# A recurrent memory layer on one core: mask by matmul, six ring slots for seventeen streamed weights, and moved loads and stores

## The chip, the cores and the metric

One core of a Trainium2 chip runs the whole program. The metric is the device time of one execution in microseconds. A core has five engines with queues of their own: TensorE (PE) for matmuls, VectorE (DVE), ScalarE (ACT), GpSimd (POOL) and SyncE (SP), which here only issues DMAs. Sixteen DMA engines move the data. An engine works through its queue in order; semaphores order the engines among each other.

## The reference

Two layers side by side. A is a dilated sliding-window attention over 2048 tokens of 640 features with 32 heads of 20. B, which takes most of the time, is a recurrence over 64 segments of 32 tokens; 8 memory tokens are carried from one segment to the next:

```python
for s in range(n_seg):                       # 64 segments, M = 8, seg_len = 32, H = 32, Dh = 192, Dm = 640
    h = jnp.concatenate([mem, xs], axis=1)   # 40 tokens
    q = jnp.einsum('btd,dhe->bhte', h, Wq)   # k, v likewise
    scores = jnp.einsum('bhqe,bhke->bhqk', q, k) * scale
    scores = jnp.where(mask[None, None], scores, -1000000000.0)
    p = _softmax(scores, axis=-1)
    o = jnp.einsum('bhte,hed->btd', jnp.einsum('bhqk,bhke->bhqe', p, v), Wo)
    mem = o[:, :M, :]                        # into the next segment
    outs.append(o[:, M:, :])
```

The mask is causal for the 32 tokens of the segment; memory tokens see everything. All 40 x 640 outputs of a segment hang on the memory of the segment before, so segments run one after another.

## The kernel before

Layer A runs first, with some preparation for B between its blocks (`between`). Then the parts of B that need no memory are computed for all segments at once: of the 32 tokens of a segment, 24 are projected inside the loop together with the 8 memory tokens (that makes 32 rows), and the 8 others, the "left" tokens, are projected ahead of it into DRAM scratch (qk_scr, v_scr). Then comes the loop over the 64 segments, and a tail that multiplies the left tokens' head outputs (ol_scr) by Wo.

The loop's weights are cut into 64 units of 128 x 1920 bf16 (480 KB): Q, K and V have 16 each, rows r = 0 to 3 by columns j = 0 to 3, and O has 16. 48 stay in SBUF; 16 are streamed in every segment: the units j = 3 of Q, K and V, out of the scratch ws_scr, and four O units straight from B_Wo. They go through a ring of five slots (N_RING; four in `temp`, one in `ring4`); SLOT gives the slot of each in order of use. When PE has used a unit, `done` issues on SP the load of the next unit for that slot (L575).

`SegmentLoop` takes operations in the order in which they are written (`op(engine, reads, writes, emit)`), works out which waits are needed between engines from the names read and written, and emits one loop body. Each engine's order in the loop is thus the order of the calls from L747 on. What `also` names is waited for as if written, and counts as read.

One segment, with lines:
- `proj` (L592): one row r of Q, K or V, 20 matmuls for the four column groups, 32 rows of HT (the transposed input) against 384 columns; ACT or DVE copies the result out of PSUM (L600), PE transposes it (`turn`, L612), and ACT and DVE write it into QT and KT (L618).
- `load_left` (L624): the left tokens' Q and K come from qk_scr by SP, and POOL copies the Q part into place (L625). The destination of K and the places PT and PTL lie in XL, where several short-lived pieces share space: OT[0], OT[1] (head outputs) and OL (the left tokens' head outputs) lie over QT and KT.
- `scores` (L651): t = 0 takes the heads of rows 0 and 1, t = 1 those of rows 2 and 3. `softmax_1` on DVE: scale and mask (L662), maximum (L665), difference (L666). `softmax_2` on ACT: exp (L670). `softmax_3` on DVE: sums, reciprocal, products (L673 to L679). `turn_p` transposes P (L688, L690; out by L692, L693), `pv` multiplies by V (L709, L714), `heads_out` (L721) and `left_out` (L725) copy out of PSUM.
- the store of OL for both halves by ACT's queue (L801), ahead of the last O units.
- `o_units` (L739): 16 units of 12 matmuls each, added up in Y.
- the turn: DVE adds the next segment's 24 tokens to Y in z (L804; `rows` is 1 on memory rows and 0 elsewhere), transposes z into HT (L806), ACT writes Y into z with zeros on memory rows (`toks`, L807), and ACT's queue stores z (L808). The next tokens come into z by four DMAs on SP (L756) out of x_scr, a copy of B's input.

Order of the segment's second half:

```python
    softmax_3(1)
    o_units(0, 0, 3)
    turn_p(1)
    o_units(0, 3, 5)
    pv(1)
    ...
    left_out(1)
    op("ACT", ["OT0.l", "OT1.l"] + QPARTS[0] + QPARTS[1], [], lambda s: nc.scalar.dma_start(ol_scr[:, s], OL), dma="ol")
    o_units(0, 5, 8)
    o_units(1, 0, 8)
```

Of the kernel before, what the change touches and what calls it, by code (L numbers as in the profile page):

```python
# [338 lines left out]
def part_b(ctx, tc, B_x, B_mem0, B_Wq, B_Wk, B_Wv, B_Wo, out, ident, bdf, run_a):  # L339
# [41 lines left out]
    ws_scr = {u: dram.tile([128, US], BF16, name=f"ws_{u[0]}_{u[1]}_{u[2]}") for u in streamed if u[0] != O}  # L381
    x_scr = dram.tile([n_seg + 1, SEG, Dm], BF16, name="x_scr")
# [21 lines left out]
    def between(i, ps):  # L404
        if i == 1:
            turn_left(ps)
            nc.sync.dma_start(x_scr[0:n_seg].rearrange("s t d -> (s t d)").rearrange("(p n) -> p n", p=128),
                              B_x.rearrange("b s d -> (b s d)").rearrange("(p n) -> p n", p=128))
            nc.sync.dma_start(x_scr[n_seg:n_seg + 1], x3[0:1])
# [76 lines left out]
    ring4 = keep3.tile([128, US], BF16, name="ring4")[:]  # L486
    vss += [ring4[:, 384 * k:384 * k + 384] for k in range(5)]
    z = keep3.tile([128, 160], BF16, name="z")
    z0 = z
    for g in range(4):  # L490
        nc.sync.dma_start(z0[32 * g:32 * g + NX, :], x_scr[0, 0:NX, 160 * g:160 * g + 160])
        nc.sync.dma_start(z0[32 * g + NX:32 * g + 32, :], mem2[:, 160 * g:160 * g + 160])
    left_v(3)
    ws_ring = [temp[:, US * k:US * k + US] for k in range(4)] + [ring4]
    for k in range(4):
# [8 lines left out]
    rows, toks = bdf[:, 3:4], bdf[:, 4:5]  # L504
# [6 lines left out]
    OL = XLb[:, 0:2 * KO].rearrange("p (t n) -> p t n", t=2)[:, :, 4 * PW:5 * PW]  # L511
# [12 lines left out]
    for g in range(2):  # L524
        m = mask[64 * g:64 * g + 64]
        nc.gpsimd.affine_select(out=m[:, 0:NX], in_=m[:, 0:NX], compare_op=ALU.is_ge, fill=-1e9, base=0,
                                pattern=[[-1, NX]], channel_multiplier=1)
        nc.gpsimd.affine_select(out=m[:, 32:L], in_=m[:, 32:L], compare_op=ALU.is_ge, fill=-1e9, base=-NX,
                                pattern=[[0, NL]], channel_multiplier=1)
        m = mask[64 * g + 32:64 * g + 64, :]  # L530
        nc.gpsimd.affine_select(out=m[:, 32:L], in_=m[:, 32:L], compare_op=ALU.is_ge, fill=-1e9, base=0,
# [14 lines left out]
    nc.gpsimd.memset(z[:], 0.0)  # L546
# [5 lines left out]
    QPARTS = [["Q.a0", "Q.a1", "Q.l"], ["K.a0", "K.a1", "K.l"]]  # L552

# [81 lines left out]
    def scores(t):  # L635
        Sps = logits(t)

        def emit(s):
# [9 lines left out]
            seen = set()  # L648
            last = {p[4]: n for n, p in enumerate(pl)}
            for n, (_, lo, rr, j, e, cc, hi) in enumerate(pl):  # L650
                i = MM(Sps[64 * e:64 * e + 64, 4 * rr + j, :], lhsT=XLb[lo:hi, L * (4 * cc + j):L * (4 * cc + j) + 64],  # L651
                       rhs=KT[lo:hi, 4 * cc + j], start=(e not in seen), stop=(n == last[e]),
                       tile_position=(lo, 64 * e))
                seen.add(e)
# [5 lines left out]
    def softmax_1(t):  # L660
        Sps = logits(t)
        op("DVE", [f"b{SB[t]}"], ["t1"], lambda s: V_.scalar_tensor_tensor(  # L662
            out=t1[:], in0=Sps, scalar=scale, in1=mask.unsqueeze(1).to_broadcast([128, 8, L]),
            op0=ALU.mult, op1=ALU.add))
        op("DVE", ["t1"], ["mx"], lambda s: V_.tensor_reduce(out=mx, in_=t1[:], axis=AX.X, op=ALU.max))  # L665
        op("DVE", ["t1", "mx"], ["t1"], lambda s: V_.tensor_tensor(  # L666
            t1[:], t1[:], mx.unsqueeze(2).to_broadcast([128, 8, L]), op=ALU.subtract))

    def softmax_2(t):
        op("ACT", ["t1"], ["t1"], lambda s: nc.scalar.activation(t1[:], t1[:], ACTF.Exp))  # L670
# [48 lines left out]
    def heads_out(t, j):  # L719
        e = ("ACT", "DVE")[j % 2]  # L720
        op(e, [f"b{4 + j}"], [f"OT{t}.{j}"], lambda s: COPY[e](  # L721
            OT[t][:, 6 * j:6 * j + 6], ots[j].rearrange("p r x l -> p (r x) l")[:, :, 0:32]), also=QPARTS[t])

    def left_out(t):
        op("DVE", [f"b{4 + j}" for j in range(4)], [f"OT{t}.l"], lambda s: nc.vector.tensor_copy(  # L725
            OL[:, t].rearrange("p (j a k) -> p j a k", j=4, k=NL),
# [187 lines left out]
```

## Time and profile before

| | |
|---|---|
| time, median of 4 runs | 2352.89 us (2336.99 to 2355.78) |
| the profiled execution | 2333.68 us, its span 2331.5 us |
| mean granted PE clock | 0.938 |
| busy, share of the span | PE 76%, DVE 41%, ACT 30%, POOL 2% |
| moved by DMA | 611.24 MB, mean 262 GB/s |
| first to last L804 (63 segments) | 489.3 to 2252.1 us |
| ahead of the loop, behind it | about 460 us, about 80 us |

How to read it: a row of a group or of the timeline has the line, the engine, the operation, out<-in with the program's names, shapes and a count. PE is the matmuls and PEld the weight loads; SPq and ACTq are the queues of SP and ACT when they issue DMAs. In brackets or behind "<-" stands how long the engine was idle before and what ended that. A row of a stretch of time has its length, the busy us of PE, PEld, DVE, ACT and POOL, the granted PE clock (1.00 is full), the share of time for which the DMA engines were busy, and GB/s. The chain that ended last is no help here: 76% of it is "issue", time in which the profile shows no wait, because the loop's waits compare with registers. The waits between engines are shown nevertheless, and they are used instead.

### The profile page before, as it was taken

How to read it: one execution, taken by the hardware profiler on the slowest of the kernel's cores; microseconds unless marked ns; L12 is line 12 of the kernel's file. 1: busy time of each engine (PE TensorE's matmuls, PEld its weight loads, DVE VectorE, ACT ScalarE, POOL GpSimd, SP SyncE). 2: the span in 40 equal slices, each digit the busy share in tenths (PEclk: the TensorE clock that was granted, in tenths of full speed). 3: DMA queues.
4: the chain of work that ended last, by engine and by line, in shares of the span. 5: the costliest groups of instructions: out<-in, count | busy, mean ns of one | idle time of the engine just before them, and what ended most of it. 6: DMA issues, size and time to landing. Idle time of an engine off the chain costs nothing.

```text
span 2331.5 us, 108118 instructions
## 1 busy us (share of the span) xinstructions
PE 1778.5 (76%) x45948; PEld 1120.5 (48%) x45948; DVE 963.1 (41%) x2284; ACT 689.9 (30%) x1633; POOL 50.3 (2%) x150
## 2 busy tenths in 40 slices
PE   7796858777777777877777778777777777777759
PEld 5442423345544445555544455444555544545436
DVE  3666312234444444444444444444444444444430
ACT  4342312222333222332232233332332322323321
POOL 0000000000000000000000000000000000000000
PEclk9899979889999999899999999999999999999989
DMA  8030975788988888888898888888898888988981
GB/s 230 22 99 23 194 226 176 244 270 300 311 293 305 296 288 287 294 297 304 293 311 294 288 305 291 293 305 291 295 308 300 292 298 295 313 292 291 303 312 62
DMA packets 259558, 611.24 MB, mean 262 GB/s; under 512 B 90608, under 2 KB 120432, under 8 KB 256768
## 3 DMA queue, kind: packets, MB, share of 16 engines
q1 hardware_dynamic: 223872, 591.35, 76.1%
q10 hardware_dynamic: 35648, 19.34, 2.8%
q8 instruction: 29, 0.48, 0.1%
q14 instruction: 9, 0.07, 0.0%
HBM read 573.62 MB, written 39.62 MB: 263 GB/s over the span
## 4 chain that ended last, share of the span: by engine, by line
issue 76%; PE 12%; DMA 7%; DVE 2%; ACT 1%; POOL 1%; POOLq 0%; ACTq 0%; SPq 0%; DVEq 0%
PE pq L75 3%; PE ps L444 3%; PE yp L836 2%; DMA temp<-in_B_Wk_dram 1%; DMA v_scr<-abc 1%; DMA ws<-temp 1%; POOL XL L625 1%; PE oT L162 1%; DVE pv L157 1%; PE ps L458 1%; PE po L87 1%; DMA temp<-in_B_Wo_dram 1%; DMA v_scr<-ring 1%; DMA v_scr<-t 1%; PE pp L141 0%
## 5 line engine op out<-in xcount | busy, mean ns | idle before, releaser
L592 PE MATMUL bank<-temp,XL 128*32 128x384 bf16 x3200 | 648.9, 342 | 0.0
L592 PE MATMUL bank<-w,XL 128*32 128x384 bf16 x7680 | 530.6, 347 | 50.4 <-DMA temp<-ws 49.8
L592 PE MATMUL bank<-wq,XL 128*32 128x384 bf16 x3840 | 272.8, 346 | 216.7 <-DMA temp<-ws 203.1
L600 ACT CAST abc<-bank 128x384 bf16<-128x384 f32 x512 | 239.2, 479 | 591.0 <-PE bank L592 585.8
L592 PEld LDWEIGHTS bank<-w,XL 128*32 128x32 bf16 x7680 | 244.6, 101 | 219.9 <-DMA temp<-ws 69.8
L592 PEld LDWEIGHTS bank<-temp,XL 128*32 128x32 bf16 x3200 | 282.1, 100 | 0.0
L592 PEld LDWEIGHTS bank<-wq,XL 128*32 128x32 bf16 x3840 | 115.6, 99 | 325.4 <-DMA temp<-ws 261.4
L618 DVE COPY XL<-bank 128x384 bf16<-128x384 bf16 x256 | 91.1, 356 | 351.0 <-PE bank L612 201.6
L739 PE MATMUL bank<-w,XL 128*32 128x160 bf16 x9216 | 231.5, 236 | 2.3 <-issue 2.3
L600 DVE CAST abc<-bank 128x384 bf16<-128x384 f32 x256 | 141.7, 554 | 212.8 <-PE bank L592 212.5
L651 PE MATMUL bank<-XL 128*64 128x40 bf16 (+1 forms) x4096 | 125.2, 190 | 98.0 <-POOL XL L625 98.0
L739 PEld LDWEIGHTS bank<-w,XL 128*32 128x32 bf16 x9216 | 173.3, 98 | 20.3 <-issue 4.2
L651 PEld LDWEIGHTS bank<-XL 128*64 128x64 bf16 (+1 forms) x4096 | 108.1, 114 | 141.1 <-POOL XL L625 131.3
L618 ACT COPY XL<-bank 128x384 bf16<-128x384 bf16 x256 | 122.4, 478 | 175.0 <-PE bank L612 98.9
L721 ACT CAST XL<-bank 128x192 bf16<-128x192 f32 x256 | 81.4, 318 | 230.7 <-PE bank L714 153.4
L721 DVE CAST XL<-bank 128x192 bf16<-128x192 f32 x256 | 91.2, 356 | 138.8 <-ACT XL L721 138.8
L592 PE MATMUL bank<-ring,XL 128*32 128x384 bf16 x640 | 146.5, 367 | 0.0
L612 PE MATMUL bank<-ident,abc 128*128 128x128 bf16 x1536 | 139.1, 231 | 0.0
L612 PEld LDWEIGHTS bank<-ident,abc 128*128 128x128 bf16 x1536 | 92.6, 102 | 89.2 <-issue 45.8
L662 DVE SCALAR_TENSOR_TENSOR t<-bank,XL 128x320 f32<-128x320 f32 x128 | 63.0, 492 | 117.7 <-PE bank L651 117.7
L688 PE MATMUL bank<-ident,t 128*128 128x128 bf16 x256 | 36.8, 226 | 62.8 <-DVE t L679 62.8
L625 POOL COPY XL<-XL 128x192 bf16<-128x192 bf16 x128 | 44.4, 347 | 1747.3 <-DMA XL<-qk_scr 1747.3
(111 smaller groups left out, 2041.3 us busy)
## 6 DMA issues: line engine op xcount, KB each, us to landing
temp<-ws SPq DMA_DIRECT2D x644, 480.0 KB, 5.0
temp<-in_B_Wo_dram SPq DMA_DIRECT2D x196, 480.0 KB, 5.2
ring<-ws SPq DMA_DIRECT2D x129, 480.0 KB, 6.1
ring<-in_B_Wo_dram SPq DMA_DIRECT2D x64, 480.0 KB, 4.0
qk_scr<-st SPq DMA_DIRECT2D x2, 6144.0 KB, 17.3
XL<-qk_scr SPq DMA_DIRECT2D x128, 96.0 KB, 4.3
abc<-v_scr SPq DMA_DIRECT2D x64, 96.0 KB, 4.0
ol_scr<-XL ACTq DMA_DIRECT2D x64, 96.0 KB, 6.7
```

Source lines behind the costliest of these rows:

```text
L75: nc.tensor.matmul(pq[32 * dd:32 * dd + 32, :], lhsT=w[:, 4 * c + dd, :], rhs=xT[:, dc, :], start=(dc == 0), stop=(dc == 4), tile_position ...
L444: nc.tensor.matmul(ps[:], lhsT=w[:, dc, o:o + 128], rhs=XL[:, dc], start=(dc == 0), stop=(dc == 4))
L592: i = MM(ps[32 * j:32 * j + 32, :], lhsT=HT[:, dc, :], rhs=ws[j][:, dc, :], start=(dc == 0), stop=(dc == 4), tile_position=(0, 32 * j))
L600: op(e, [f"b{b}"], [f"abc{k}"], lambda s: COPY[e](ABC[k], bank[b][:, 0:384]))
L612: i = nc.tensor.transpose(tp[ty][:, c], ABC[nat[ty, r]][:, 128 * c:128 * c + 128], ident)
L618: op(e, [("b3", "b5")[ty]], [QPARTS[ty][h]], lambda s: COPY[e](QT[:, 12 * h:12 * h + 12, 0:32] if ty == Q else KT[:, 12 * h:12 * h + 12, 0:4],
L625: op("POOL", ["PT", "PTL"], ["Q.l"], lambda s: nc.gpsimd.tensor_copy(QT[:, :, 32:L], ql))
L651: i = MM(Sps[64 * e:64 * e + 64, 4 * rr + j, :], lhsT=XLb[lo:hi, L * (4 * cc + j):L * (4 * cc + j) + 64], rhs=KT[lo:hi, 4 * cc + j], start ...
L662: op("DVE", [f"b{SB[t]}"], ["t1"], lambda s: V_.scalar_tensor_tensor(out=t1[:], in0=Sps, scalar=scale, in1=mask.unsqueeze(1).to_broadcast( ...
L721: op(e, [f"b{4 + j}"], [f"OT{t}.{j}"], lambda s: COPY[e](OT[t][:, 6 * j:6 * j + 6], ots[j].rearrange("p r x l -> p (r x) l")[:, :, 0:32]), ...
L739: i = MM(Y[32 * g:32 * g + 32], lhsT=OT[t][:, 6 * j + 3 * rr + x], rhs=w[:, x, 160 * g:160 * g + 160], start=(t == 0 and n == 0 and x == 0 ...
L836: nc.tensor.matmul(yp[h][:], lhsT=OL[tb][:, 24 * (r // 2) + 6 * j + 3 * (r % 2) + x].rearrange("p s l -> p (s l)"), rhs=w[:, x, 320 * h:32 ...
```

## The change

- Mask: a matmul of the identity with the mask (its fill divided by scale) writes the mask into the scores' PSUM ahead of the products; the DVE operation of L662 goes, maximum and difference read PSUM, and exp gets scale.
- Ring: six slots and 17 streamed units (12 of Q, K, V and five of O, another choice of them); one O unit fewer stays in SBUF. ws_scr's rows stand 4096 instead of 3840 bytes apart.
- OL: the first half stays in XL and is stored behind V of row 3, the second half lies in t1 and is stored alone. `OPARTS` leaves K's left part out of what OT[1] waits for.
- Order: `load_left(0)` moves to the front of the segment, `load_left(1)` behind the first scores, five O units stand ahead of turn_p(1) and three behind it.
- z: x_scr holds the tokens in z's layout with zeros on memory rows, one DMA per segment loads it, ACT copies Y as it is (`toks` goes), and SP stores z.

```diff
-    streamed = [u for u in order if u[0] != O and u[2] == 3 or u in ((O, 0, 2), (O, 0, 3), (O, 2, 1), (O, 2, 3))]
-    N_STR, N_RING = 16, 5
-    SLOT = [0, 1, 2, 3, 0, 4, 1, 2, 0, 3, 4, 1, 0, 2, 3, 4]
+    streamed = [u for u in order if u[0] != O and u[2] == 3 or u in ((O, 1, 0), (O, 0, 3), (O, 2, 0), (O, 2, 2), (O, 3, 3))]
+    N_STR, N_RING = 17, 6
+    SLOT = [0, 1, 2, 3, 4, 5, 0, 2, 1, 3, 4, 0, 2, 1, 3, 4, 5]
...
-    ws_scr = {u: dram.tile([128, US], BF16, name=f"ws_{u[0]}_{u[1]}_{u[2]}") for u in streamed if u[0] != O}
-    x_scr = dram.tile([n_seg + 1, SEG, Dm], BF16, name="x_scr")
+    ws_scr = {u: dram.tile([128, 2048], BF16, name=f"ws_{u[0]}_{u[1]}_{u[2]}")[:, 0:US] for u in streamed if u[0] != O}
+    x_scr = dram.tile([n_seg + 1, 128, 160], BF16, name="x_scr")
...
+            zero = lx.tile([n_seg + 1, NL * 160], BF16, name="zero")
+            nc.gpsimd.memset(zero[:], 0.0)
+            for g in range(4):
+                nc.sync.dma_start(x_scr[0:n_seg, 32 * g:32 * g + NX, :], x3[:, 0:NX, 160 * g:160 * g + 160])
+                nc.sync.dma_start(x_scr[n_seg:n_seg + 1, 32 * g:32 * g + NX, :], x3[0:1, 0:NX, 160 * g:160 * g + 160])
+                nc.scalar.dma_start(x_scr[:, 32 * g + NX:32 * g + 32, :].rearrange("s t n -> s (t n)"), zero[:])
...
-    OL = XLb[:, 0:2 * KO].rearrange("p (t n) -> p t n", t=2)[:, :, 4 * PW:5 * PW]
+    OL = [XLb[:, 4 * PW:5 * PW], t1b[:, 256:256 + PW]]
...
+            for e in range(2):
+                h = slice(64 * e, 64 * e + 64)
+                MM(Sps[h], lhsT=ident[h, h], rhs=mask[h].unsqueeze(1).to_broadcast([64, 8, L]), start=True, stop=False,
+                   tile_position=(64 * e, 64 * e), skip_group_check=True)
...
-        op("DVE", [f"b{SB[t]}"], ["t1"], lambda s: V_.scalar_tensor_tensor(
-            out=t1[:], in0=Sps, scalar=scale, in1=mask.unsqueeze(1).to_broadcast([128, 8, L]),
-            op0=ALU.mult, op1=ALU.add))
-        op("DVE", ["t1"], ["mx"], lambda s: V_.tensor_reduce(out=mx, in_=t1[:], axis=AX.X, op=ALU.max))
+        op("DVE", [f"b{SB[t]}"], ["mx"], lambda s: V_.tensor_reduce(out=mx, in_=Sps, axis=AX.X, op=ALU.max))
...
+    load_left(0)
     qk(Q, 0)
     qk(K, 0)
     qk(Q, 1)
-    load_left(0)
...
+    op("SP", [], ["z"], lambda s: nc.sync.dma_start(z[:], x_scr[s + 1]), dma="xz")
     qk(K, 2)
     scores(0)
+    load_left(1)
     softmax_1(0)
     qk(Q, 3)
-    load_left(1)
...
+    op("ACT", ["OT0.l"] + QPARTS[0], [], lambda s: nc.scalar.dma_start(ol_scr[:, s, 0], OL[0]), dma="ol0")
     softmax_3(1)
-    o_units(0, 0, 3)
+    o_units(0, 0, 5)
     turn_p(1)
-    o_units(0, 3, 5)
+    o_units(0, 5, 8)
     pv(1)
...
+    op("ACT", ["OT1.l", "t1"], [], lambda s: nc.scalar.dma_start(ol_scr[:, s, 1], OL[1]), dma="ol1")
-    o_units(0, 5, 8)
     o_units(1, 0, 8)
...
-    op("ACT", ["b2"], ZG, lambda s: nc.scalar.activation(z[:], Y, ACTF.Copy, scale=toks))
-    op("ACT", ZG, [], lambda s: nc.scalar.dma_start(out3[s], z[:]), dma="yo")
+    op("ACT", ["b2"], ["z"], lambda s: nc.scalar.copy(z[:], Y))
+    op("SP", ["z"], [], lambda s: nc.sync.dma_start(out3[s], z[:]), dma="yo")
```

More of the change, by code (lines that the diff above doesn't have):

```diff
@@ L502, in part_b @@
     psum = lctx.enter_context(tc.tile_pool(name="b_ps", bufs=1, space=PSUM))
-    rows, toks = bdf[:, 3:4], bdf[:, 4:5]
+    rows = bdf[:, 3:4]
     XLb = XL[:].rearrange("p c s l -> p (c s l)")
@@ L545, in part_b @@
     nc.vector.transpose(HT.rearrange("p c t -> p (c t)"), z[:])
-    nc.gpsimd.memset(z[:], 0.0)
     lp = SegmentLoop(nc, tc, n_seg)
@@ L552, in part_b @@
     QPARTS = [["Q.a0", "Q.a1", "Q.l"], ["K.a0", "K.a1", "K.l"]]
+    OPARTS = [QPARTS[0], QPARTS[1][:2]]
     def source(u):
@@ L651, in emit @@
                 i = MM(Sps[64 * e:64 * e + 64, 4 * rr + j, :], lhsT=XLb[lo:hi, L * (4 * cc + j):L * (4 * cc + j) + 64],
-                       rhs=KT[lo:hi, 4 * cc + j], start=(e not in seen), stop=(n == last[e]),
-                       tile_position=(lo, 64 * e))
-                seen.add(e)
+                       rhs=KT[lo:hi, 4 * cc + j], start=False, stop=(n == last[e]),
+                       tile_position=(lo, 64 * e), skip_group_check=True)
             return i
@@ L742, in emit @@
                 return i
-            op("PE", [f"OT{t}.{j}", wkey(u)] + QPARTS[t], ["b2"], emit)
+            op("PE", [f"OT{t}.{j}", wkey(u)] + OPARTS[t], ["b2"], emit)
             done([u])
-    ZG = [f"z.{g}" for g in range(4)]
+    load_left(0)
     qk(Q, 0)
@@ L754, in part_b @@
     qk(K, 1)
-    for g in range(4):
-        op("SP", [], [ZG[g]], lambda s, g=g: nc.sync.dma_start(
-            z[32 * g:32 * g + NX, :], x_scr[s + 1, 0:NX, 160 * g:160 * g + 160]), dma="xz")
     qk(Q, 2)
```

44 lines of the change are left out of this document (19 added, 25 removed).

## The prediction

> **What bounds the kernel now.** First I read how long one turn of the loop takes. The row of the line that ends a segment (count, shortest/median/longest ns, first and last start), the engines' busy time between those two starts, and the answer on waits for the same stretch:
>
> ```profile
> L804 DVE SCALAR_TENSOR_TENSOR z<-bank,bdf,z x64: 382/384/386, 489.3 to 2252.1; 128x160 bf16<-128x160 f32 x64
> 489.30:2252.10 1762.80, 1347.74 (x42210) 884.68 (x42210) 754.06 (x2017) 532.00 (x1323) 43.73 (x126) 0.95 0.87 297
> PE bank L592 <- DMA temp<-ws: 252.9, 207, 2.6
> PE bank L651 <- POOL XL L625: 94.9, 98, 2.4
> PE bank L688 <- DVE t L679: 61.6, 52, 1.2
> PE bank L592 <- DVE XL L806: 4.2, 4, 1.0
> ```
>
> Between the first and the last L804 lie 63 segments: 1762.8/63 = **27.98 us** each. The first engine column is PE: 1347.74/63 = 21.39 us busy; the four waits are 413.6/63 = 6.57 us, and the two make up the segment. So PE is the thread to follow: it is never idle for another reason, and a saving counts only if it comes out of these 6.57 us: 4.08 for loads (with the 4.2 of L806), 1.51 for the 8 "left" tokens, 0.98 for the softmax. DVE (12.0 us) and ACT (8.4) are no bound. DMA is: its share is 0.87 at 297 GB/s, so a segment moves 297 x 27.98 = 8.31 MB.
>
> Part of the 4.08 us isn't a load at all. At a segment's turn (start, us taken, engine, line, idle before):
>
> ```profile
> 1216.73 0.38 DVE L804 SCALAR_TENSOR_TENSOR z<-bank,bdf,z 128x160 bf16<-128x160 f32 x1 [0.77 <-PE bank L739]
> 1217.15 0.34 DVE L806 STREAM_TRANSPOSE XL<-z 128x160 bf16<-128x160 bf16 x1
> 1217.62 0.34 PE L592 MATMUL bank<-wq,XL 128*32 128x384 bf16 x3 [1.04 <-DVE XL L806]
> ```
>
> Y, the add, the transpose and Q of row 0 are one chain of 1.04 us; the change leaves it. So 3.04 us per segment are real waits for loads. Then I looked at who holds the loads up, in SyncE's queue of the next segment and its waits, with two DMA stretches:
>
> ```profile
> 1216.14 0.39 ACTq L801 DMA_DIRECT2D ol_scr<-XL  x1
> 1218.65 2.23 SPq L575 DMA_DIRECT2D temp<-ws  x3
> 1223.66 0.58 SPq L624 DMA_DIRECT2D XL<-qk_scr  x1
> 1224.38 0.50 SPq L575 DMA_DIRECT2D temp<-ws  x1
> 1226.67 1.84 SPq L756 DMA_DIRECT2D z<-x_scr  x4
> SPq L624 <- DMA ol_scr<-XL: 80.0, 55, 2.5
> 1227.50:1229.50 2.00, 1.87 (x53) 1.32 (x54) 0.85 (x2) 0.00 (x0) 0.08 (x1) 1.00 0.16 40
> 1238.50:1239.50 1.00, 1.00 (x45) 0.78 (x37) 0.62 (x3) 0.75 (x3) 0.00 (x0) 1.00 0.10 38
> ```
>
> The store of OL (L801) is issued when the segment is nearly over, and the next segment's left load (L624) may not overwrite its source. It goes out at 1223.66, and the weight load queued behind it at 1224.38. Three microseconds later the DMA engines stand at 0.16 for 2 us. At 1238.5 they are empty again because all five slots are full and wait for PE. Every such hole is paid back at the next dense stretch, as waits of PE.
>
> **The change, part by part.** *Left loads and OL.* OL splits: its first half is stored after V, its second half lies in t1, so no Q/K destination waits for the store, and the left loads go ahead of Q of row 0 and right behind the first scores.
>
> ```profile
> 1200.47 0.94 PE L651 MATMUL bank<-XL 128*64 128x40 bf16 x32 [0.74 <-POOL XL L625]
> 1201.34 0.34 PE L592 MATMUL bank<-wq,XL 128*32 128x384 bf16 x3
> 1201.51 0.33 PE L592 MATMUL bank<-wq,XL 128*32 128x384 bf16 x3
> 1202.89 0.58 SPq L624 DMA_DIRECT2D XL<-qk_scr  x1
> 1207.00 0.35 POOL L625 COPY XL<-XL 128x192 bf16<-128x192 bf16 x1 [6.58 <-DMA XL<-qk_scr]
> 1207.40 0.94 PE L651 MATMUL bank<-XL 128*64 128x40 bf16 x32 [1.24 <-POOL XL L625]
> ```
>
> The second load has 1207.00 - 1202.89 = 4.11 us until POOL copies, and 0.40 more until PE. Issued at about 1201.6, behind the scores instead of Q of row 3, it lets PE start at 1206.1; PE would be ready at 1207.40 - 1.24 = 1206.16. The first gains several us. So 1.51 falls to about 0.1: **-1.4**. Its bounds are -1.5 and the rival below in which the loads land late.
>
> *Softmax and order.* The mask goes into PSUM by PE, DVE loses L662, and five instead of three O units stand ahead of turn_p(1), three instead of two ahead of pv(1), none between pv(1) and the second half.
>
> ```profile
> 1208.38 0.49 DVE L662 SCALAR_TENSOR_TENSOR t<-bank,XL 128x320 f32<-128x320 f32 x1 [0.77 <-PE bank L651]
> 1208.90 0.49 DVE L665 TENSOR_REDUCE XL<-t 128x8 f32<-128x320 f32 x1
> 1213.78 0.40 PE L714 MATMUL bank<-XL,abc 32*64 32x32 bf16 x24
> 1214.25 0.32 ACT L721 CAST XL<-bank 128x192 bf16<-128x192 f32 x1 [0.98 <-PE bank L714]
> 1214.54 0.80 PE L739 MATMUL bank<-w,XL 128*32 128x160 bf16 x36
> 1215.16 0.38 PE L739 MATMUL bank<-temp,XL 128*32 128x160 bf16 x12
> ```
>
> L662 and its hand-over are 0.52 us (1208.90 - 1208.38); a unit is (1215.16 - 1214.54)/3 = 0.21, two are 0.41. Together 0.93 of the 0.98 us for L679. But the units behind pv(1) covered ACT's copy: pv ends at 1214.18, the copy at 1214.57, and with 0.13 of hand-over (as from 1217.49 to 1217.62 above) PE will stand 0.52 us there. Net **-0.4** (bounds: -0.98, and +0.1 if DVE is slower on PSUM; L662 read PSUM at the same 0.49, so I see no reason).
>
> *Mask by PE.* Two 64x64 matmuls of 320 columns per scores. The nearest rows are the projections: four 384-column matmuls on four column groups start every 1201.51 - 1201.34 = 0.17 us. Side by side a pair costs 320/384 x 0.17 = 0.14, one behind another 0.28. I take 0.17: **+0.35** per segment (0.28 to 0.56).
>
> *Six slots and a seventeenth unit.* What moves now (sizes, median us to landing) and what the engines reach when they have work:
>
> ```profile
> temp<-ws SPq DMA_DIRECT2D x644, 480.0 KB, 5.0
> temp<-in_B_Wo_dram SPq DMA_DIRECT2D x196, 480.0 KB, 5.2
> ring<-ws SPq DMA_DIRECT2D x129, 480.0 KB, 6.1
> ring<-in_B_Wo_dram SPq DMA_DIRECT2D x64, 480.0 KB, 4.0
> XL<-qk_scr SPq DMA_DIRECT2D x128, 96.0 KB, 4.3
> 1192.50:1196.50 4.00, 2.37 (x46) 1.22 (x46) 1.36 (x3) 0.96 (x2) 0.00 (x0) 1.00 1.01 395
> 1231.50:1238.50 7.00, 5.20 (x177) 3.54 (x181) 3.30 (x10) 1.57 (x4) 0.35 (x1) 1.00 0.97 362
> ```
>
> The 1033 loads are 16 per segment and nine outside. One more is 0.49 MB: 8.31 becomes 8.80 MB. At 395 GB/s that takes 22.3 us, at 362 (seven us with the small transfers in it) 24.3. PE alone, with no wait for a load, would need 27.98 - 3.04 - 1.4 - 0.4 + 0.35 - 0.2 (the clock, below) = 23.3 us. So **DMA becomes the bound, just ahead of PE.** Six slots for 17 units mean each waits 6/17 of a segment between refills, against 5/16 now: at 24.8 us the same 8.75 us that it has today. I take 24.3 plus 0.2 of collisions: 1.2 us of load waits stay, **-1.85**.
>
> *SyncE's queue.* The store of z moves from ACT to SP and waits there for ACT's copy at the turn; behind it stand the left load and the load that Q of row 0 frees. That one goes out about 0.7 us later and has over 5 us until row 3 needs it: nothing. The z load is one instead of four DMAs (1.84 us of SP) and waits for the store to land; behind it is O33's load, needed last. Nothing, up to +0.3.
>
> *The clock.* Two stretches, the granted clock third from the end:
>
> ```profile
> 1132.80:1160.80 28.00, 20.90 (x707) 13.96 (x700) 12.28 (x33) 8.49 (x22) 0.69 (x2) 1.00 0.88 300
> 1104.90:1132.80 27.90, 22.87 (x602) 13.79 (x594) 11.12 (x30) 8.11 (x20) 0.69 (x2) 0.82 0.85 283
> ```
>
> At full clock PE needs 20.90 us for the same work, against the mean of 21.39. With less idle I take **-0.2** of that 0.5. The Trainium skill (TensorE: Matmul & The Clock Gate, Part 1: The HAM clock gate) says that the gate opens with activity and halves the clock after an idle window; by it nearly all of the 0.5 us would go, and the sum would be some 20 us lower.
>
> *Outside the loop.* x_scr is written in rows of 320 bytes by eight DMAs plus four of zeros on ACT, in a stretch where DMA idles:
>
> ```profile
> 60.00:100.00 40.00, 29.49 (x177) 11.64 (x177) 26.13 (x18) 11.65 (x20) 0.00 (x0) 0.79 0.02 9
> PE yp L836 <- ACT w L829: 20.5, 1, 20.5
> ```
>
> I count 0 (-5 for fewer z loads ahead of the loop, +10 if SP or ACT is held). The tail's fifth O unit loads under the 20.5 us that PE waits there for OL.
>
> **Sum:** 27.98 - 1.4 - 0.4 + 0.35 - 1.85 - 0.2 = 24.5 us; 3.48 x 64 = 223 us off the profiled execution's 2333.68 (span and launch), 2111. The median of the runs, 2352.89, is 1.0082 times that: **2128 us**.
>
> **The rivals.** (Times in the scale of the median.)
> - *The ring hides all* (0.15): 23.3 us a segment, 300 us less, 2050. For it: DMA reached 395. Against: only in stretches of 4 us.
> - *The seventeenth unit eats what the ring gives* (0.18): the 3.04 us of load waits stay; 27.98 - 1.4 - 0.4 + 0.35 - 0.2 = 26.3, 105 us less, 2246. For it: four DMAs in flight to the same engines, landing 5 us after issue.
> - *DMA is full already* (0.08), the slower side: if 297 GB/s is what this mixture can do, 8.80 MB take 29.6 us, 106 us more, 2459. It decides from a rate below 8.80/27.98 = 315 GB/s. Against: the holes at 0.10 and 0.16, which are no limit of DMA.
> - *The left load lands late* (0.07): it stands in SP's ring behind weight loads issued earlier, more of them than now. Three more at 0.49 MB/395 = 1.24 us and it lands 8.0 us after issue, 2.9 beyond its cover: 27.4, 37 us less, 2315. Near no change.
> - *Padded rows read slower* (0.02). ws_scr rows go from 3840 to 4096 bytes apart, 13 of 17 units. At half the rate 13 x 1.24 = 16 us more per segment, over 3000 us. No row of before has such a pitch. The Trainium skill (DMA: Bandwidth & Descriptors, Latency and other measured facts) speaks against powers of two as pitch, from 512 KiB up, 207 GB/s against 214 and 103 at worst; 4 KiB isn't in its list, and by its smallest figure this would be some 35 us.
>
> **How the numbers follow.** The forecast has 0.5. Its own range is 24.5 +- 0.8, 2075 to 2180. The range holds it and the two faster and weaker cases: 2035 to 2260; outside are part of the first rival and the last three. Changes under 1% can't be told from none here. Faster by more: 0.50 + 0.15 + 0.18 and part of the late left load, 0.86; slower 0.10; between 0.04.
>
> **What would show it.** L651 waits for POOL below 0.2 us a segment; no wait of L618 or L624 for ol_scr; L688's wait gone, and a new one at the first O unit behind pv(1) of about 0.5; DMA near 360 GB/s with a share over 0.93; load waits of 1.2 us beside the turn. Wrong it would be if the share rose while GB/s didn't, or if SP stood at the store or load of z for over 1 us with weight loads behind it.

## The result: 2206 us, 5.9% faster, and the profile after

| | before | after |
|---|---|---|
| median of the runs | 2344.67 us (15 runs, 2327.49 to 2368.93) | 2205.83 us (10 runs, 2202.37 to 2214.37) |
| ratio, 95% interval | | 0.9415 [0.9389, 0.9440] |
| the profiled execution | 2333.68 us | 2209.42 us, its span 2207.4 us |
| one segment | 27.98 us | 25.80 us |

The forecast was 2128 us, in a range of 2035 to 2260. The sign and the range hold. The gain is 139 us where 225 was forecast. For e10 below, the four slowest of its ten executions (2342.74 to 2354.82 us) are left out of the time, and since its profile is of the slowest of them, its rows are an upper end.

The same rows as before, now of the kernel after. First the row of the line that ends a segment (L804 before, L803 now), by line:

```profile
L803 DVE SCALAR_TENSOR_TENSOR z<-bank,bdf,z x64: 383/384/384, 498.0 to 2123.1; 128x160 bf16<-128x160 f32 x64
```

Then the stretch between its first and its last start (length, busy us of PE, PEld, DVE, ACT and POOL, granted clock, DMA share, GB/s):

```profile
498.00:2123.10 1625.10, 1343.96 (x42462) 897.54 (x42462) 709.36 (x1890) 529.30 (x1323) 43.96 (x126) 0.97 0.95 342
```

And PE's waits in it (line and what it waited for: us in all, times, longest):

```profile
PE bank L595 <- DMA temp<-ws: 95.2, 118, 1.8
PE bank L653 <- POOL XL L628: 66.7, 75, 1.3
PE bank L595 <- DVE XL L805: 62.5, 61, 1.0
PE bank L741 <- ACT XL L723: 32.4, 63, 0.5
PE bank L690 <- DVE t L681: 17.3, 42, 0.4
PE bank L595 <- DMA ring<-ws: 4.9, 14, 1.1
```

1625.1/63 = 25.80 us per segment. PE is busy for 21.33 of it, so the two kernels need the same PE time; what went is waiting. The loads' rows fell from 252.9 to 100.1 us (95.2 and 4.9) and the softmax's from 61.6 to 17.3. A new row appeared (L741, 32.4), the copy behind pv(1). The row of the turn, L805, shows its whole 62.5 us now, since no load hides it any more. But the row that the forecast had nearly gone, the left tokens by way of POOL, only fell from 94.9 to 66.7.

SyncE's queue shows where that comes from. The timeline of SP around the second left load (L627) of a segment, then POOL's copy and PE's first matmul with what arrived:

```profile
1201.88 0.37 SPq L578 DMA_DIRECT2D ring<-in_B_Wo_dram  x1
1203.01 0.57 SPq L627 DMA_DIRECT2D XL<-qk_scr  x1
...
1209.88 0.35 POOL L628 COPY XL<-XL 128x192 bf16<-128x192 bf16 x1 [8.29 <-DMA XL<-qk_scr]
...
1210.28 0.32 PE L653 MATMUL bank<-XL,ident 64*64 64x320 bf16 x2 [1.10 <-POOL XL L628]
```

The left load goes out right behind the load of O(3,3), the unit that is needed last of all, and takes 6.87 us until POOL copies. PE stood ready at 1209.18 (1210.28 - 1.10); with 0.40 from the copy to PE, a landing by 1208.78, 5.77 us after issue, would have cost nothing. The DMA answer and two stretches of the same segment:

```profile
ring<-ws SPq DMA_DIRECT2D x194, 480.0 KB, 6.3
XL<-qk_scr SPq DMA_DIRECT2D x128, 96.0 KB, 5.4
```

```profile
1202.00:1212.00 10.00, 7.44 (x233) 4.92 (x233) 4.54 (x12) 3.00 (x7) 0.35 (x1) 1.00 1.03 401
1213.00:1215.00 2.00, 2.00 (x32) 0.95 (x28) 1.55 (x6) 1.16 (x3) 0.00 (x0) 0.50 0.28 86
```

A left load of 96 KB takes 5.4 us now, against 4.3 before, because it is issued into a stretch in which the engines are full (share 1.03, 401 GB/s). One microsecond after that stretch the same engines stand at 0.28: SP issues no load from 1209.29 to 1213.97, since no slot comes free. So the transfer that PE waits for runs beside transfers that nobody needs yet, and then there is nothing to move. The granted clock in that second stretch is 0.50: a projection's matmuls start every 0.32 us there (1213.07, 1213.39), against 0.17 at full clock (1203.30, 1203.47). So PE, which has just waited, also empties the slots at half the pace.

### The profile page after: what moved, and what is told of

Read it like the earlier page. It is cut to its first block, busy times and chain, and to the rows that moved or that the text cites. A ratio compares the mean times of both kernels' runs of the same rounds, so it can differ in the third digit from the quotient of the medians.

```text
span 2207.4 us, 108320 instructions
## 1 busy us (share of the span) xinstructions
PE 1776.8 (80%) x46204; PEld 1138.2 (52%) x46204; DVE 917.6 (42%) x2155; ACT 687.4 (31%) x1633; POOL 51.3 (2%) x150
## 4 chain that ended last, share of the span: by engine, by line
issue 43%; PE 24%; DMA 22%; ACT 4%; DVE 4%; POOL 2%; ACTq 1%; SPq 0%; POOLq 0%; DVEq 0%
DMA ol_scr<-XL 13%; PE bank L595 5%; PE pq L75 3%; PE bank L657 3%; PE yp L835 2%; PE ps L447 2%; DMA temp<-ws 2%; POOL XL L628 2%; DMA w<-in_B_Wv_dram 2%; PE bank L711 2%; DMA v_scr<-abc 2%; DMA w<-in_B_Wk_dram 1%; PE ps L461 1%; DVE pv L157 1%; PE po L87 1%
## 5 line engine op out<-in xcount | busy, mean ns | idle before, releaser
L595 PE MATMUL bank<-temp,XL 128*32 128x384 bf16 x2880 | 568.3, 340 | 0.0
L595 PEld LDWEIGHTS bank<-w,XL 128*32 128x32 bf16 x7680 | 247.2, 101 | 235.8 <-DMA temp<-ws 89.3
L595 PE MATMUL bank<-wq,XL 128*32 128x384 bf16 x3840 | 255.4, 329 | 107.6 <-DVE XL L805 62.5
L595 PEld LDWEIGHTS bank<-temp,XL 128*32 128x32 bf16 x2880 | 259.3, 99 | 0.0
L741 PE MATMUL bank<-w,XL 128*32 128x160 bf16 x8448 | 216.9, 235 | 0.0
L595 PE MATMUL bank<-ring,XL 128*32 128x384 bf16 x960 | 204.4, 347 | 0.0
L741 PEld LDWEIGHTS bank<-w,XL 128*32 128x32 bf16 x8448 | 163.7, 98 | 17.9 <-issue 4.5
L615 PE MATMUL bank<-ident,abc 128*128 128x128 bf16 x1536 | 131.9, 223 | 0.0
L667 DVE TENSOR_REDUCE XL<-bank 128x8 f32<-128x320 f32 x128 | 62.9, 492 | 108.8 <-PE bank L657 108.8
L741 PE MATMUL bank<-temp,XL 128*32 128x160 bf16 x2304 | 74.9, 236 | 34.0 <-ACT XL L723 34.0
L653 PE MATMUL bank<-XL,ident 64*64 64x320 bf16 x256 | 41.4, 320 | 67.8 <-POOL XL L628 66.9
```

The lines of the kernel that those rows point to most:

```text
L595: i = MM(ps[32 * j:32 * j + 32, :], lhsT=HT[:, dc, :], rhs=ws[j][:, dc, :], start=(dc == 0), stop=(dc == 4), tile_position=(0, 32 * j))
L615: i = nc.tensor.transpose(tp[ty][:, c], ABC[nat[ty, r]][:, 128 * c:128 * c + 128], ident)
L667: op("DVE", [f"b{SB[t]}"], ["mx"], lambda s: V_.tensor_reduce(out=mx, in_=Sps, axis=AX.X, op=ALU.max))
L741: i = MM(Y[32 * g:32 * g + 32], lhsT=OT[t][:, 6 * j + 3 * rr + x], rhs=w[:, x, 160 * g:160 * g + 160], start=(t == 0 and n == 0 and x == 0 ...
```

## The experiments

**The theories.** A: the loop is bound by DMA's bytes, 8.80 MB per segment, and a byte saved is time saved. B: the order in the queues and the distances in the ring set the waits; bytes matter only through them. A2 says of B that O(3,3)'s load ahead of the left load is the one that matters, and C that it is the number of units between two uses of a slot.

All variants below carry one more instruction on POOL and on PE ahead of the left tokens' work and the scores, and their wait registers start 4096 higher. e0 is the kernel after with only that, and **each variant is read against e0**. The lines of the variants are one to six higher than in the kernel after. The variants ran in three groups (e0, e1, e3, e4; then e2, e5, e7, e8; then e6, e9, e10, e11), in which the kernel before had medians of 2330.08, 2339.63 and 2335.08 us; so differences of some 0.4% between groups say nothing.

### e0: the control

```diff
-                    E[e].reg_mov(regs[key], total[p])
+                    E[e].reg_mov(regs[key], total[p] + 4096)
...
+                    if waits[n] and (eng == 'POOL' or eng == 'PE' and 'scores' in emit.__qualname__):
+                        E[eng].sem_inc(spare[eng], 1)
```

> The changed kernel itself; only, in the loop, an increment of an unused semaphore stands between the waits and the first instruction of scores and of POOL's copy, and the registers that waits compare with start 4096 higher. It is the base for the other variants. Expected by every theory: the changed kernel's 2206 us within 0.5%, since two increments of some 0.05 us per segment on PE are 6 us at most.

Measured: 2226.84 us, 0.9541 [0.9477, 0.9606] of before; 26.02 us per segment. Its stretch and its waits:

```profile
502.60:2141.80 1639.20, 1350.45 (x42462) 904.21 (x42462) 709.15 (x1891) 527.95 (x1323) 43.73 (x126) 0.96 0.94 339
```

```profile
PE bank L598 <- DMA temp<-ws: 90.1, 114, 1.9
PE bank L656 <- POOL XL L631: 79.2, 84, 1.4
PE bank L693 <- DVE t L684: 16.9, 41, 0.4
```

It is 21 us (0.95%) over the kernel after, outside the 0.5% that was expected; PE's busy time is up by 6.5 us and the wait for the left tokens by 12.5. Which of the added instructions does it isn't known. The picture is the same, so it serves as the base.

### e4: O(3,3) loaded later

```diff
-    def done(us):
+    def done(us, late=False):
...
-            if u in pos:
+            if u in pos and (late or u != (K, 2, 3)):
...
     proj(V, 1)
+    done([(K, 2, 3)], late=True)
```

The bytes stay. Only the refill of the slot that K of row 2 frees goes out behind V of row 1, no longer ahead of the left load.

> The changed kernel with one load moved: the load of O unit (3,3), which is needed last in the segment, is issued behind V of row 1 instead of behind K of row 2, so out of the dense stretch of Q and K and into the stretch in which the DMA engines run empty. Theory A2 (bound by DMA in the dense stretch, while it stands idle later in the segment): 1.0 us a segment less, 64 us, about 2140 us, left and load waits both smaller. Theory A1 (bound by the mean rate of DMA): 2206, no change. Rival B (order of left loads behind weights): the left load has one weight load fewer ahead of it, 1.2 us earlier, its wait goes, 0.9 us a segment, 2150; then the waits for weight loads stay as they are.

Measured: 2139.22 us, 0.9169 [0.9107, 0.9232]; 24.61 us per segment. Its stretch, its waits, and SP and POOL at the second left load:

```profile
500.80:2051.20 1550.40, 1313.39 (x42462) 883.18 (x42462) 709.10 (x1891) 520.16 (x1323) 44.03 (x126) 0.99 0.99 359
```

```profile
PE bank L598 <- DMA temp<-ws: 102.7, 140, 1.4
PE bank L598 <- DVE XL L809: 62.8, 61, 1.0
...
PE bank L656 <- POOL XL L631: 6.0, 17, 0.7
```

```profile
1199.63 0.57 SPq L630 DMA_DIRECT2D XL<-qk_scr  x1
...
1205.40 0.35 POOL L631 COPY XL<-XL 128x192 bf16<-128x192 bf16 x1 [7.28 <-DMA XL<-qk_scr]
1207.61 2.98 SPq L581 DMA_DIRECT2D ring<-in_B_Wo_dram  x2
```

One load, issued 8 us behind the left load and no longer 1.1 us ahead of it, takes 88 us off the time. The left load reaches POOL in 5.77 us, and its wait falls from 79.2 to 6.0 us in all, 1.16 us per segment. PE's busy time falls by 37.1 us, 0.59 per segment, with the clock at 0.99 instead of 0.96. The load waits stay (102.7 against 90.1). A2 has the time, but not its smaller load waits. B has both waits right, and its 2150 us lies inside the interval as well. With the share at 0.99 the engines have no hole left: 359 GB/s x 24.61 us = 8.83 MB, the bytes of the forecast. This is the fastest version here that computes the whole output. It beats both kernels, and comes within 0.11 us of the segment (24.5 us) and 3 GB/s of the rate (362) that the prediction worked out for the change itself. The edit takes the load out of the queue ahead of the left load and out of the dense stretch at once; which of the two counts isn't separated here.

### e1: sixteen units, six slots

```diff
-    streamed = [u for u in order if u[0] != O and u[2] == 3 or u in ((O, 1, 0), (O, 0, 3), (O, 2, 0), (O, 2, 2), (O, 3, 3))]
-    N_STR, N_RING = 17, 6
-    SLOT = [0, 1, 2, 3, 4, 5, 0, 2, 1, 3, 4, 0, 2, 1, 3, 4, 5]
+    streamed = [u for u in order if u[0] != O and u[2] == 3 or u in ((O, 1, 0), (O, 0, 3), (O, 2, 0), (O, 2, 2))]
+    N_STR, N_RING = 16, 6
+    SLOT = [0, 1, 2, 3, 4, 5, 0, 2, 1, 3, 4, 0, 2, 1, 3, 4]
...
+        if u == (O, 3, 3):
+            res[u] = res[O, 3, 2]
...
```

O(3,3) isn't loaded; O(3,2) stands in for it.

> The changed kernel with 16 streamed units in six slots: the last O unit (3,3) isn't loaded; the product uses the resident unit (3,2) in its place, so the output differs there. 0.49 MB per segment less to move. Theory A (the DMA engines are the bound at about 342 GB/s): 0.49/342 = 1.43 us a segment less, 92 us, so about 2115 us. Rival B (PE waits for order: the left loads behind weight loads in SP's queue, and the turn; the amount of bytes matters little): the left and load waits stay, at most 0.3 us a segment less, 2185 us or more.

Measured: 2159.35 us, 0.9255 [0.9183, 0.9327]; 24.95 us per segment. Stretch and waits:

```profile
502.60:2074.30 1571.70, 1326.29 (x42462) 897.61 (x42462) 708.54 (x1891) 527.96 (x1323) 43.73 (x126) 0.98 0.93 334
```

```profile
PE bank L659 <- POOL XL L634: 77.5, 63, 1.4
...
PE bank L601 <- DMA temp<-ws: 47.5, 73, 1.5
```

67 us less, between the theories. The load waits halve (90.1 to 47.5), so bytes seem to count; but slot 5 now holds one unit alone, which also gives K of row 2 a whole segment for its load. The wait for the left tokens stays (77.5), although O(3,3) is gone: slot 5 is now refilled with K of row 2 for the next segment, from the same place in the queue. e4, with all the bytes, is 20 us faster. Both edits at once weren't tried.

### e3: left loads from ACT's queue

```diff
-        op("SP", [], ["K.l", "PT", "PTL"], lambda s: nc.sync.dma_start(left, qk_scr[:, :, t, s, :]), dma="qkl")
+        op("ACT", [], ["K.l", "PT", "PTL"], lambda s: nc.scalar.dma_start(left, qk_scr[:, :, t, s, :]), dma="qkl")
```

> The changed kernel with both left loads issued from ACT's queue instead of SP's, at the same places of the program. Theory A (DMA is the bound): the left loads land earlier, the 1.06 us for which PE waits on POOL fall to 0.3 or less, but the same bytes are moved and the weight loads come later by as much; 2195 us, within 1% of the control. Rival B (the queue order is the fault): 0.8 us a segment less, 51 us, about 2155 us.

Measured: 2249.31 us, 0.9646 [0.9575, 0.9718]. Both expectations were too low. Waits of PE, and the DMA row of the left loads (5.3 us in e0):

```profile
PE bank L656 <- POOL XL L631: 148.2, 85, 2.8
...
PE bank L598 <- DMA temp<-ws: 28.0, 57, 1.1
```

```profile
XL<-qk_scr ACTq DMA_DIRECT2D x128, 96.0 KB, 6.3
```

Another queue doesn't let the left load pass. It lands later (6.3 us), the wait for it nearly doubles, and the weight loads gain most of what it loses (90.1 to 28.0).

### e2: the old ring in the new kernel

```diff
-    N_STR, N_RING = 17, 6
-    SLOT = [0, 1, 2, 3, 4, 5, 0, 2, 1, 3, 4, 0, 2, 1, 3, 4, 5]
+    N_STR, N_RING = 16, 5
+    SLOT = [0, 1, 2, 3, 0, 4, 1, 2, 0, 3, 4, 1, 0, 2, 3, 4]
...
```

The four streamed O units are those of before too.

> The control with the old ring: five slots and the old 16 streamed units, all else as changed. One unit less to move (the 16 units in six slots took 67 us off the control), but one slot fewer. Theory A2 (bound by DMA in the dense stretch, and there what is queued ahead of the left loads and of Q3 and K3 decides): the old slots load no unit in the dense stretch that isn't needed soon, so the ring's seventeenth unit brought little; 2190 to 2230 us. Rival (the sixth slot is the gain of the change): 26.3 us a segment or more as in the prediction's second rival, 2260 us or more.

Measured: 2329.68 us, 0.9966 [0.9934, 0.9999]; 27.81 us per segment. A2's 2190 to 2230 is missed by 100 us, and the rival holds. So everything in the change but the ring is worth 0.17 us per segment by itself (0.39 with the 0.22 by which e0's segment is longer than that of the kernel after), where the prediction's steps for it add up to 1.65. Stretch, waits, and the timeline at the worst of them, Q of row 2:

```profile
497.20:2249.50 1752.30, 1420.19 (x42462) 922.43 (x42462) 704.87 (x1890) 523.86 (x1323) 43.73 (x126) 0.92 0.89 300
```

```profile
PE bank L598 <- DMA temp<-ws: 232.6, 103, 4.4
...
PE bank L693 <- DVE t L684: 22.9, 57, 0.4
...
PE bank L656 <- POOL XL L631: 6.4, 20, 0.7
```

```profile
1221.98 0.59 SPq L630 DMA_DIRECT2D XL<-qk_scr  x1
1222.70 2.76 SPq L581 DMA_DIRECT2D temp<-ws  x4
...
1227.24 0.34 PE L598 MATMUL bank<-wq,XL 128*32 128x384 bf16 x3 [2.14 <-DMA temp<-ws]
```

The waits for the left tokens and for the softmax go (6.4 and 22.9 us), as forecast, and the load wait stays: 232.6 us, against 252.9 in the kernel before. All in all PE is idle for less: 1752.30 - 1420.19 = 332 us, where it was 1762.80 - 1347.74 = 415, so 1.32 us per segment are saved. What takes them back is PE's busy time, 1.15 us per segment more than before: 0.38 for the mask (e8), and 0.77 with the clock at 0.92 instead of 0.95. That isn't chance: the mean granted clock of e2's ten executions is 0.905 to 0.914, and of the thirteen of the kernel before beside them 0.935 to 0.952.

Why the load wait stays: in the old ring Q of row 2 uses the slot that Q of row 0 has just left, four units earlier. Its load, the first of the four at 1222.70, can't go out before that, and stands behind the left load, which this change moved to the segment's front. PE is there first, whatever else became quicker. The load waits are fewer than before and longer (103 of 2.3 us on average against 207 of 1.2).

### e9: six slots, short distances

```diff
-    SLOT = [0, 1, 2, 3, 4, 5, 0, 2, 1, 3, 4, 0, 2, 1, 3, 4, 5]
+    SLOT = [0, 1, 2, 3, 0, 4, 1, 2, 0, 3, 4, 1, 5, 2, 3, 4, 5]
```

The 17 units and six slots stay, with the old reuse in the Q and K part (four units from Q of row 0 to Q of row 2, against five or more in the change).

> The control with 17 units and six slots, but the slots of Q, K and V as in the old ring: slot 0 is used again after four units (Q of row 0, Q of row 2, V of row 0) instead of five or more, and slot 5 holds two O units. As many bytes and slots as the control; only the distance between two uses of a slot in the dense stretch differs. Theory C (what decides is the distance: a load takes 5 to 6 us from issue to landing, longer than PE takes for the four units in between, which also is why the old ring gave 2330): about 27.5 us a segment, 2300 us or more, with PE waiting at Q of row 2. Rival (the number of slots, so the capacity, is what the ring brings): 2227 us within 1%.

Measured: 2371.66 us, 1.0172 [1.0097, 1.0247]: the whole gain of the change is gone. One segment is 28.35 us. Waits, and PE at the fifth projection of a segment that began at 1215.69:

```profile
PE bank L598 <- DMA temp<-ws: 153.8, 64, 4.8
PE bank L744 <- DMA ring<-in_B_Wo_dram: 92.4, 63, 2.5
```

```profile
1222.93 0.34 PE L598 MATMUL bank<-wq,XL 128*32 128x384 bf16 x3 [1.80 <-DMA temp<-ws]
```

C holds. With the same bytes, the same number of slots and the same order of work on PE, the list of slots alone is worth 145 us against e0: 1.40 us per segment of waits, and 0.93 of PE's busy time at a clock of 0.93 instead of 0.96. Part of it is a second short distance that I had overlooked: O(1,0) and O(3,3) share slot 5 four streamed units apart, the 92.4 us. The list also sets when each refill can go out, so the distance and the place in SP's queue change together.

### e5: a quarter of the bytes

```diff
-                op("SP", [], [wkey(u)], lambda s, u=u, k=k: nc.sync.dma_start(ws_ring[slot(u)], source(streamed[k])), dma=wkey(u))
+                op("SP", [], [wkey(u)], lambda s, u=u, k=k: nc.sync.dma_start(ws_ring[slot(u)][:, 0:480], source(streamed[k])[:, 0:480]), dma=wkey(u))
```

Three quarters of every streamed unit stay as they were; the number of DMAs is the same.

> The control with every streamed load in the loop cut to a quarter of its columns (480 of 1920; the rest of a slot keeps what was there, so the output differs). As many DMAs, rows and waits, a quarter of the weight bytes. Theory A2: the load waits (1.52 us a segment) and the left waits (1.26) go, and the clock rises; about 22.9 us a segment instead of 26.0, 200 us less, about 2030 us. Rival B (order of issue and waits, not bytes): at most 1 us a segment less, 2165 us or more.

Measured: 1979.34 us, 0.8465 [0.8413, 0.8517]; 22.24 us per segment. Its stretch, and the row of the left loads:

```profile
495.40:1896.50 1401.10, 1278.03 (x42462) 887.62 (x42462) 703.85 (x1891) 519.22 (x1323) 43.74 (x126) 1.00 0.41 115
```

```profile
XL<-qk_scr SPq DMA_DIRECT2D x128, 96.0 KB, 2.4
```

All of PE's waits:

```profile
PE bank L598 <- DVE XL L808: 65.0, 63, 1.0
PE bank L744 <- ACT XL L726: 32.2, 63, 0.5
PE bank L693 <- DVE t L684: 25.9, 63, 0.4
```

No wait for a load or for the left tokens is left; the left loads land in 2.4 us. So with this number of DMAs and semaphores PE needn't wait, and the bytes make the waits that e0 has. The time is 50 us below A2's 2030, and rival B is out. PE's own chain is 22.24 us, below the 23.3 that the prediction gave it, mostly since the clock stays at 1.00: PE is busy for 20.29 us, where 21.54 were forecast.

### e7 and e11: the old order of the O units

```diff
-    o_units(0, 0, 5)
+    o_units(0, 0, 3)
     turn_p(1)
-    o_units(0, 5, 8)
+    o_units(0, 3, 5)
     pv(1)
...
+    o_units(0, 5, 8)
     o_units(1, 0, 8)
```

> The control with the O units in their old places: three ahead of turn_p(1), two behind it, three behind pv(1). By the prediction's step the wait for the softmax grows by 0.41 us (from 0.27) and the wait behind pv(1) of 0.51 goes: together -0.1 us a segment, 2220 us, no difference that can be told. If the order was a gain of its own, +0.4 us a segment, 2253 us.

> Two variants in one: the load of O unit (3,3) behind V of row 1 (2139 us alone) and the O units in their old places (2215 us alone, 12 below the control). If PE's own chain still counts, 8 to 12 us less than with the moved load alone, about 2129 us; theory A2 with the DMA engines now busy for nearly all of the time: 2139, no difference.

Measured: e7 2214.94 us, 0.9468 [0.9410, 0.9525], no difference from e0 that the intervals tell; e11, this edit on top of e4, 2151.42 us, 0.9233 [0.9191, 0.9276], none from e4. The one median is 12 us lower than its base, the other, for which 2129 or 2139 was expected, 12 us higher. The softmax's row of e7:

```profile
PE bank L693 <- DVE t L684: 35.6, 43, 0.8
```

It rises from 16.9 to 35.6, and the 32 us behind pv(1) go. The order exchanges one wait for another.

### e8: the mask by DVE again

The diff is the mask's part of the change, reversed: two matmuls per scores go, and DVE has its multiply-add back.

> The control with the mask back on DVE: no matmul of the mask, scale and mask by one more DVE operation ahead of the maximum. By the prediction's step DVE's chain is 0.52 us longer and PE has 0.35 us less work: the wait for the softmax grows from 0.27 to about 0.8; +0.2 us a segment, 2240 us. Theory A2 with DMA as the bound: much of it is hidden, 2227 to 2240. If the mask by PE was a loss: 2205.

Measured: 2229.67 us, 0.9520 [0.9458, 0.9581], as e0. Its stretch:

```profile
500.30:2144.80 1644.50, 1326.25 (x42210) 898.00 (x42210) 762.72 (x2016) 527.61 (x1323) 44.01 (x126) 0.96 0.94 338
```

PE is busy for (1350.45 - 1326.25)/63 = 0.38 us less per segment, and the time is the same, since PE waits 0.47 us longer. Half of that is the softmax's row, which rises from 16.9 to 31.6 us because DVE has its operation back:

```profile
PE bank L694 <- DVE t L685: 31.6, 42, 0.8
```

Of the three forecasts 2205 is out; 2240 and "hidden" can't be told apart within this interval.

### e6: the old row pitch

```diff
-    ws_scr = {u: dram.tile([128, 2048], BF16, name=f"ws_{u[0]}_{u[1]}_{u[2]}")[:, 0:US] for u in streamed if u[0] != O}
+    ws_scr = {u: dram.tile([128, US], BF16, name=f"ws_{u[0]}_{u[1]}_{u[2]}") for u in streamed if u[0] != O}
```

> The control with ws_scr's rows 3840 bytes apart again. If the padding changes nothing in how rows are read: 2227 us within 0.5%. If padded rows read slower, as the prediction's last rival has it, 20 us less or more; if faster, 2245 or more.

Measured: 2230.03 us, 0.9553 [0.9507, 0.9599], as e0. Between rows 4096 and 3840 bytes apart no difference shows. The Trainium skill (DMA: Bandwidth & Descriptors, Latency and other measured facts) warns of powers of two as pitch from 512 KiB up; at 4 KiB this run shows nothing of it.

### e10: the old path of z

```diff
-    op("SP", ["z"], [], lambda s: nc.sync.dma_start(out3[s], z[:]), dma="yo")
...
+    op("ACT", ZG, [], lambda s: nc.scalar.dma_start(out3[s], z[:]), dma="yo")
```

With it come back the plain x_scr, four z loads per segment and the scaling of Y by `toks`.

> The control with the path of z undone: x_scr as a plain copy of the input, four z loads per segment, zeros written by ACT, the store of z from ACT's queue. The prediction counted 0 for the loop and 0 (-5 to +10) outside it. By the two profiles the loop starts some 9 us later with the change and the rest of the loop is unmoved: about 2219 us here, 8 less than the control. If the store and load of z on SP hold up weight loads, 20 us less or more than that; if the four loads were a cost, 2240 or more.

Measured: 2327.08 us as the median of six executions, 0.9956 [0.9907, 1.0005]. That is 100 us above e0, where 2219 had been expected: the widest miss of all. SP's wait at the z load (33.4 us in the kernel before, 6.0 after), PE's for the left tokens, then ACT and SP in one segment:

```profile
SPq L763 <- DMA out_dram<-z: 168.0, 59, 4.5
```

```profile
PE bank L654 <- POOL XL L629: 204.7, 63, 5.1
```

```profile
1202.07 0.57 ACTq L811 DMA_DIRECT2D out_dram<-z  x1
...
1211.59 1.84 SPq L763 DMA_DIRECT2D z<-x_scr  x4
1213.54 0.37 SPq L579 DMA_DIRECT2D ring<-in_B_Wo_dram  x1
1214.15 0.58 SPq L628 DMA_DIRECT2D XL<-qk_scr  x1
```

The z load may overwrite z only when the store has landed. The store, 40 KB from ACT's queue, holds it until 1211.59, 9.5 us after its issue, and behind the z load stand O(3,3)'s load and the left load. The row tells that the store is what SP waits for; its queue and the four-part load weren't undone one by one, so their shares stay open.

## Why the prediction was right and wrong, by its own steps

Per segment, from the rows of the kernel after:

| step | forecast | measured |
|---|---|---|
| left tokens (1.51 before) | 0.1 | 66.7/63 = 1.06 |
| waits for loads, without the turn's 1.04 (3.04 before) | 1.2 | (95.2 + 4.9 + 62.5)/63 - 1.04 = 1.54 |
| softmax and the new wait behind pv(1) (0.98 before) | 0.05 + 0.52 | 0.27 + 0.51 |
| mask by PE | +0.35 | +0.38 (e8) |
| PE busy, mask and clock in it | 21.54 | 21.33 |
| segment | 24.5 | 25.80 |
| outside the loop, in all | 0 | +13.6 |

**The step that failed is the left load's**, 0.96 of the 1.3 us. It gave the second load the 4.11 us that it had before, at an earlier place in the queue, and priced its landing at before's load. In the same text the ring was made to fill the engines, and the two steps were never put together: a fuller ring makes every landing longer, 5.4 us in place of 4.3, and O(3,3)'s new load stands right in front. The rival "the left load lands late" named the mechanism. Its size was wrong: 8.0 us to landing, where the second load reached POOL after 6.87 us in the segment shown. By its own rows its cover was 1206.16 - 0.40 - 1201.6 = 4.2 us, so that 8.0 would lie 3.8 beyond it and not 2.9. e4 moves O(3,3)'s load and leaves 6.0 us of this wait, e5 cuts the bytes and leaves none; e2, with the old ring, brings the step's whole (94.9 - 6.4)/63 = 1.40 us. So the step holds beside the old ring, where the left loads land in 3.6 us and PE, held by weight loads, also comes later; with the fuller ring most of it is lost.

**Load waits** (1.54 for 1.2): near the mark for the change, but not for the reason given. "DMA becomes the bound at 362 GB/s" is what e4 reaches; the kernel after gets 342, since its engines still run dry (0.28) behind the stretch in which PE waited for one late transfer. The prediction's count of slots, 6/17 of a segment each, was the wrong measure. e9 has the same count and takes 145 us more: what counts is how many streamed units lie between two uses of a slot, where they are fewest.

**Softmax and order**: the waits fell by 0.2 where 0.4 was forecast; the 0.52 behind pv(1) came as 0.51. In e7 and e11 the order is worth nothing that can be measured. **Mask**: +0.35 was right as PE time. With the 0.52 us that it takes off DVE's chain the forecast for the mask as a whole was a gain of 0.17 us per segment, 11 us in all, which is less than e8 can show. Both steps were summed as if PE were the only thread, although the same text had just made DMA the bound; whether DMA hides them, e8 and e11 leave open.

**The sum itself** is the second thing to correct. The steps aren't additive: e2 removes the left and softmax waits and gains 0.17 to 0.39 us, where 1.65 was forecast for all but the ring. Its waits do fall, by 1.32 us; but the load waits, which stay, come in fewer and longer pieces, and the granted clock falls with it. That the clock could go down with a step was in no term of the sum.

**The rivals on the ring**: the seventeenth unit has a price (67 us, e1) but doesn't eat all that the ring gives, and the ring can't hide everything, as 359 GB/s at a share of 0.99 (e4) leaves the engines no more room.

**The clock**: -0.2 was forecast, out of 0.5 us that were to be had. Both were too small. The prediction's two stretches don't hold the same work (707 and 602 matmuls, where a segment of the kernel before has 42210/63 = 670). In e5, at 1.00 throughout, PE is busy for 20.29 - 0.38 = 19.91 us without the mask, so of the 21.39 before, 1.48 us belonged to the clock. In the kernel after 0.44 of them came (21.33 - 0.38 = 20.95), in e4, at 0.99, 0.92, and in e2, at 0.92, PE lost 0.77. The Trainium skill's rule (TensorE: Matmul & The Clock Gate, Part 1: The HAM clock gate) says that activity opens the gate and an idle window closes it. That the clock rises as waits go, as in e4 and e5, agrees with it better than my 0.2 does. How long an idle window has to be, these rows don't show: in the kernel after, PE has no wait over 1.8 us. The sum of the waits isn't what decides, though: PE was idle for 6.59 us per segment at 0.95 before, and for 5.27 at 0.92 in e2. The longest single wait orders these kernels better: 1.0 us in e5 (1.00), 1.4 in e4 (0.99), 1.8 after (0.97), 2.6 before (0.95), 4.4 in e2 (0.92) and 4.8 in e9 (0.93); e11, with 2.5 at 0.98, doesn't fit as well. No run changes the length of a wait alone, so this is a pattern and not a shown cause.

**SyncE's queue at nothing**: its waits at the new place of z's store are as forecast, 0.79 us per segment for ACT's copy and next to nothing at the z load:

```profile
SPq L807 <- ACT z L806: 49.7, 63, 0.8
SPq L760 <- DMA out_dram<-z: 6.0, 16, 0.5
```

Whether those 0.79 us cost PE anything, no run tells. That the old path of z would have cost 100 us with the fuller ring (e10) I had not seen. **Padded rows**: refuted as a rival, by e6.

**Outside the loop** the first L803 is 498.0 - 489.3 = 8.7 us later than before, and the tail 84.3 us (2123.1 to 2207.4) against 79.4. The tail's part is at its second unit, O(1,0), now streamed:

```profile
2149.66 1.76 PE L835 MATMUL yp<-temp,w 128*128 128x320 bf16 x6 [3.83 <-DMA temp<-in_B_Wo_dram]
```

The forecast hid this load behind PE's wait for OL; PE waits 3.83 us for it, of the 4.9 us by which the tail grew. The 8.7 us ahead of the loop weren't traced to a cause. Lastly, scaling by 1.0082 to the median added 17 us that the kernel after doesn't show (2209.42 profiled, 2205.83 median). Without it the forecast would have been 95 us too low, and not 78. Of the signs that the prediction named, the left wait under 0.2 us and the 360 GB/s didn't come; the wait behind pv(1) and the share over 0.93 did, and no load waits for ol_scr any more.

## What to carry to other kernels

In a ring of prefetched weights, count for each slot the streamed units between its two uses, and compare their duration with the landing time under load (medians of 5.3 to 6.3 us in the kernel after), not with the transfer's own time; slots and bytes say less. In one queue, issue loads in the order in which they are needed: one load needed last, ahead of one needed next, cost 4% here (e4). And when an edit fills the transfer engines, work out the landing of every other transfer again at that load before adding up the steps.

## What the runs showed of the hardware

- This one core kept 359 GB/s as a mean over the whole loop at a DMA share of 0.99 (e4), and 401 over 10 us (the kernel after).
- A left load of 96 KB takes 2.4 us to land where the engines are 0.41 busy (e5), 5.3 beside a full SP queue (e0), and 6.3 from ACT's queue beside the same (e3). A queue of its own was no priority for it. Why it lands later there, these runs don't separate.
- The granted clock was 0.91 to 1.00 between kernels with nearly the same matmuls, worth (1420.19 - 1278.03)/63 = 2.26 us of busy PE time per segment between e2 and e5. A wait needn't be long for it to fall: in the kernel after, where no wait of PE in the loop is over 1.8 us, it stands at 0.50 from 1213 to 1215. And less waiting in all doesn't have to raise it (e2 against before).
